# Small filler products in TensorE's gaps in the opening of a kernel of attention, SwiGLU and maxout

## The chip, the cores and the metric

The kernel runs on one core of one Trainium2 chip. The metric is the time of one execution on the device in microseconds (us). PE is TensorE's matmul, PEld its weight load, DVE is VectorE, ACT is ScalarE, POOL is GpSimd, SPq is SyncE's queue, which issues the DMA transfers.

## The reference

Three layers follow one another. The attention has 4 batches of 8 heads with 576 positions of 64 values; half of the heads see the last 32 positions, the other half every 32nd position. Its 2304 rows of 512 values go through a gated layer of width 1536 and then through a layer that takes the largest of three products of width 768.

```python
scores = scale * np.matmul(q, k.transpose(0, 1, 3, 2))
...
attn = np.exp(scores)
attn = attn / (np.sum(attn, axis=-1, keepdims=True) + 1e-09)
return np.matmul(attn, v).astype(np.float32)
...
silu = g * (1.0 / (1.0 + np.exp(-g)))
val = x @ w_val
return (silu * val @ w_out).astype(np.float32)
...
h = np.maximum(np.maximum(x @ w1, x @ w2), x @ w3)
return (h @ w_out).astype(np.float32)
```

All of it is float32. The weights arrive as 64-bit words, and a part of the kernel's work turns each of their tiles into two tiles whose sum it is; each large product is made of three products of such halves.

## The kernel before, in words

The rows are worked on in five chunks of up to 512. While the first chunk's attention is computed, the first layer's weights are still coming in and being converted; this is the opening, and it is written out by hand as a list of steps, `FIRST`. A step is a letter and a number, and each engine runs its own instructions in the order of that list. After the opening a planner orders the instructions.

The steps that matter here are those of the attention blocks. Blocks 0 to 3 belong to the strided heads and blocks 4 to 7 to the local ones. For a block n:

- `l` and `m` load its queries, keys and values; `k0` and `k1` load the constants (identity and masks).
- `Sn` makes the scores on PE: 8 products of 64 rows (line 390).
- `Mn` masks them and takes the row's extreme on DVE (L426), `En` is the exponential on ACT (L434), `Rn` the reciprocal of the sums on DVE (L439, L440), `Nn` the division on POOL (L444).
- `Tn` transposes the result on PE (L456): 2 transposes for a strided block, 4 for a local one. `Vn` copies them out of PSUM, on DVE (L463) or, for blocks 1 and 4, on ACT (L461).
- `Pn` multiplies with the values on PE (L498): 8 products. `Hn` and `Ln` split the outcome into the halves xh and xl (ACT L510 or DVE L512, and DVE L516).

The other letters are the weights' steps: `r` loads a tile, `a`, `q`, `s`, `c`, `t`, `d` convert it on ACT, POOL and DVE (L199 to L228), `h` and `o` split it (ACT L243, DVE L248). `G` and `b` are the gate's first products (L693 to L695 on `ps_g`).

PSUM has eight banks, and each of `Sn`, `Tn` and `Pn` asks for the next one in a rotation (`bank`); it waits until what was in that bank has been read. PE's order in the opening is S0 S1 S2 S3 T0 S4 T1 P0 T2 P1 S5 T3 P2 P3 S6 T4 T5 S7 P5 P4 G0 T6 T7 P6 P7, then S8 and the dense products of the first layer.

Of the kernel before, what the change touches and what calls it, by code (L numbers as in the profile page):

```python
# [7 lines left out]
F32 = mybir.dt.float32  # L8
# [44 lines left out]


FIRST = """
l0 k0 l1 l2 l3 l4 m4 k1 l5 m5 r0 l6 m6 l7 m7 r1 r2 r3 r4 S0 M0 S1 E0 M1 S2 R0 E1 N0 M2 S3 E2 R1 T0 M3 N1 S4 V0
E3 R2 T1 P0 N2 M4 V1 T2 R3 P1 E4 V2 N3 H0 S5 L0 T3 H1 M5 P2 V3 E5 L1 P3 R4 N4 H3 a0 S6 R5 q0 c0 L3 T4 H2 M6 N5
s0 t0 T5 L2 E6 S7 d0 V5 h0 M7 P5 V4 R6 E7 P4 o0 N6 G0 a1 R7 H5 N7 T6 H4 L5 a2 l8 L4 c1 T7 V6 q1 s1 r5 V7 q2 P6
c2 a3 P7 t1 H6 r6 q3 s2 L6 S8 H7 d1 s3 L7 c3 m8 h1 b0 t2 r7 a4 o1 q4 d2 a5 B0 t3 c4 r8 h2 M8 c5 u0 o2 s4 r9 w0
E8 d3 G1 x0 r10 h3 t4 t5 z0 o3 q5 y1 d4 a6 j0 s5 B1 R8 s6 l9 h4 d5 u1 r13 o4 q7 h5 N8 q6 w1 c6 O0 r12 a7 o5 s7  # L60
t6 x1 c7 m9 a8 d6 q8 r11 T8 t7 c8 z1 G2 V8 d7 h6 y3 j1 h7 o6 a9 o7 q9 r14 P8 s8 a10 c9 S9 u2 t8 l10 l11 H8 B2
s9 M9 c10 y4 L8 a11 d8 E9 w2 c11 r15 t10 O1 x2 h8 q11 R9 m10 m11 o8 z2 N9 r17 q10 t9 s11 T9 j2 G3 s10 d9 r16
t11 V9 d10 h9 d11 y7 a12 o9 h10 P9 h11 s12 B3 y6 u3 o10 H9 o11 q12 L9 c12 W10 a13 w3 y9 q13 c13 a14 t12 M10
M11 s13 x3 c14 O2 r21 q14 s14 z3 t13 E10 d12 r18 d13 G4 j3 h12 R10 h13 r19 o12 a15 N10 q15 t14 y10 a16 T10 o13
u4 B4 d14 V10 w4 c15 r20 s15 c16 t15 q16 s16 h14 y12 d15 P10 a17 o14 q17 O3 x4 c17 H10 l12 h15 t16 r23 s17 L10
z4 d16 E11 y13 o15 G5 h16 j4 q18 R11 m12 l13 m13 o16 a18 r24 s18 N11 t17 c18 a19 T11 d17 S12 u5 y15 t18 c19 B5
V11 w5 h17 M12 q19 r22 o17 a20 d18 E12 t19 s20 P11 y16 x5 G6 c20 h18 R12 H11 t20 z5 N12 s19 L11 r26 j5 q20 T12
o18 a21 O4 d20 r25 V12 d19 q21 h20 c21 h19 o20 r27 s21 t21 P12 S13 o19 a22 B6 d21 H12 l14 l15 u6 c22 L12 y19
h21 s22 w6 q22 o21 q23 r28 t22 O5 a24 x6 s23 c24 m14 m15 d22 z6 y18 q24 s24 h22 j6 a23 o22 G7 r29 a25 M13 c23
q25 t24 E13 r31 t23 c25 d24 W14 s25 d23 y21 B7 h24 R13 M14 h23 N13 u7 y22 o23 E14 w7 t25 T13 M15 r32 a26 o24  # L70
O6 V13 R14 s26 x7 q26 c26 r30 a27 N14 z7 t26 q27 d25 P13 r33 a28 j7 G8 h25 d26 H13 o25 s27 L13 c27 y24 h26 c28
t27 a29 T14 o26 q29 r34 B8 d27 V14 s28 u8 s29 c29 w8 y25 t28 h27 q28 t29 o27 a30 O7 r35 x8 s30 q30 d28 z8 y27
c30 h28 j8 a31 o28 q31 G9 d29 q32 y28 s31 c31 t30 h29 t31 E15 d30 O8 d31 u9 o29 h30 R15 h31 o30 a32 N15 y30
a33 w9 B9 s32 q33 o31 a34 c32 y31 q34 c33 s33 t32 T15 a35 x9 c34 G10 V15 t33 s34 z9 d32 q35 j9 h32 d33 s35 P14
P15 o32 u10 B10 t34 h33 w10 c35 H14 H15 d34 L14 L15 h34 o33 O9 o34 y33 x10 t35 z10 d35 y34 j10 h35 G11 o35 y35
O10 u11 w11 B11 x11 z11 j11
"""


# [14 lines left out]
def tile_attention_swiglu_maxout(  # L94
# [13 lines left out]
    nc = tc.nc  # L108
# [6 lines left out]
    def sub(stack, name, bufs, **kw):  # L115
        return stack.enter_context(tc.tile_pool(name=name, bufs=bufs, **kw))
# [9 lines left out]
    const = sub(one, "const", 1)  # L126
# [16 lines left out]
    consts = [cst[:, sum(cols[:i]):sum(cols[:i + 1])] for i in range(len(cols))]  # L143
    minus_half = const.tile([128, 1], F32, name="mh")
    nc.gpsimd.memset(minus_half, -0.5)
    ident, mask, smask = consts[0], consts[2:4], consts[1::3]
    halves = slice(0, sum(cols[:2])), slice(sum(cols[:2]), sum(cols))

# [148 lines left out]
            xt[c] = tuple(x_p.tile([128, NK, N], F32R, name=f"x{p}", tag=f"x{p}{c % 2}") for p in "hl")  # L297
        return xt[c]

    early_banks = [0]  # L300

    def claimed():
        with ExitStack() as tied:
# [5 lines left out]
    class Block:  # L309
# [8 lines left out]
            self.half = [slice(j * D, (j + 1) * D) for j in range(2)]  # L318

        def bank(self):  # L320
            if self.early:
                early_banks[0] += 1
                p, tag = ((acc, "acc"), (gv, "gv"), (acc, "acc"), (att, "att"))[early_banks[0] % 4]
            else:
                p, tag = att, "att"
            return p.tile([128, 512], F32, name="ps_a", tag=tag)
# [202 lines left out]
    def strided_block(srcs, b, g, stacked=False):  # L529

        _, rows, nr = ON_PE[b]
        assert STRIDE % nr == 0

        def dst(src, us):
            su = src.rearrange("p a (r i) -> p a r i", i=rows)
            gs = g[us]
            for c, i0, i1, o in pieces(b * NI, b * NI + rows):
                def part(t):
                    t = t[:, 2:4, :width(c)].rearrange("p a (i r) -> p a r i", r=STRIDE)
                    return t[:, :, gs[0] * nr:(gs[-1] + 1) * nr, i0:i1]  # L540

                xh, xl = x_tile(c)
                yield part(xh), part(xl), su[:, :, :, o:o + i1 - i0]

        at = g[0] // 2 if stacked else g[0]
        return Block(srcs, at, rows * nr, [smask[b]] * len(g), dst, nq=rows * nr, stacked=stacked)

    def pairs(ns):
        ns = list(ns)
        return [ns[i:i + 2] for i in range(0, len(ns), 2)]  # L550
# [89 lines left out]
    def attention_blocks(c):  # L640
        rows = ORDER[ROWS[c]:ROWS[c + 1]]
        blocks = [local_block(g) for g in joined([r // LR for r in rows[::LR]])]
        if c == 1:
            blocks += [strided_block((st1qk, st1v), 1, g) for g in pairs(range(STRIDE // ON_PE[1][2]))]
        return blocks
# [273 lines left out]
    run, h2 = {}, {}  # L919
# [93 lines left out]
    if True:  # L1013
        blocks = [strided_block((st0,), 0, g, True) for g in pairs(range(STRIDE // ON_PE[0][2]))]
        blocks += [local_block(g, (wo_p, wo_p, wo_p, wv_p)[n]) for n, g in enumerate(pairs(range(EARLY)))]
        blocks += attention_blocks(1)

        def evictor(i):
            return nc.vector if i in (0, 2, 3, 5, 6, 7) else nc.scalar

# [2 lines left out]
            "l": lambda i: blocks[i].load_qk(),  # L1023
            "m": lambda i: blocks[i].load_v(),
            "S": lambda i: blocks[i].scores(),
            "W": lambda i: blocks[i].scores_beside(blocks[i + 1]),
            "M": lambda i: blocks[i].least(),
            "E": lambda i: blocks[i].exps(),
            "R": lambda i: blocks[i].inverse(),
            "N": lambda i: blocks[i].normalise(nc.gpsimd if i < 8 else nc.vector),  # L1030
            "T": lambda i: blocks[i].turn(),
            "V": lambda i: blocks[i].evict(evictor(i)),
            "P": lambda i: blocks[i].outputs(),
            "H": lambda i: blocks[i].high(nc.vector if i in (0, 3) else nc.scalar),
# [211 lines left out]
```

## Time and profile before

| | us |
|---|---|
| median of 3 runs | 790.94 |
| lowest and highest | 790.83, 791.69 |
| the profiled execution | 791.56 |
| its span, from the first to the last instruction | 789.5 |
| PE busy in the span | 774.3 |

The profile is that of one execution. Its own time is 0.62 us above the median and 2.06 us above its span. PE busy counts a matmul from its start to its modelled end, so matmuls in a row overlap in it.

### The profile page before, as it was taken

The page shows a single profiled execution, that of the slowest core. Times are in us where ns is not written, and L with a number is a line of the kernel's source. Part 1 is how long each engine was busy: PE and PEld are TensorE (multiplying, and loading weights), DVE is VectorE, ACT ScalarE, POOL GpSimd, SP SyncE. Part 2 cuts the span into 40 slices and gives each one's busy share as a digit, 9 for nine tenths or more (in the row PEclk, how much of TensorE's full clock was granted, in tenths as well). Part 3 has the DMA queues.
Part 4 walks back from the last instruction along what each step waited for, and adds up shares of the span by engine and source line. Part 5 has one row for each costly group of instructions (what it writes and reads, how often), then busy time and mean ns, then how long its engine had stood idle before and what let it go on. Part 6 is the DMA issues. An engine that isn't in the chain of part 4 may idle for free.

```text
span 789.5 us, 13319 instructions
## 1 busy us (share of the span) xinstructions
PE 774.3 (98%) x4642; PEld 711.5 (90%) x4642; DVE 613.1 (78%) x1206; ACT 403.8 (51%) x927; POOL 231.2 (29%) x225
## 2 busy tenths in 40 slices
PE   6999999999999999999999999999999999999998
PEld 4777788888888998988999999999999999999998
DVE  5899998886799999799795778745689377856683
ACT  6899997346474637545342645433245233443331
POOL 2433342022321432324242646521124011321120
PEclk9899999999999999999999999999999999999999
DMA  9989886985846886747788999996775966878722
GB/s 292 328 287 332 300 345 235 360 269 184 276 168 222 302 294 220 250 170 255 253 274 289 302 379 384 345 383 249 274 262 196 423 254 246 286 283 344 271 96 81
DMA packets 75595, 216.26 MB, mean 274 GB/s; under 512 B 8488, under 2 KB 42024, under 8 KB 70920
## 3 DMA queue, kind: packets, MB, share of 16 engines
q1 hardware_dynamic: 75528, 215.41, 76.9%
q8 instruction: 37, 0.61, 0.3%
q14 instruction: 30, 0.25, 0.1%
HBM read 171.34 MB, written 44.04 MB: 273 GB/s over the span
## 4 chain that ended last, share of the span: by engine, by line
PE 79%; DVE 11%; ACT 6%; DMA 2%; issue 2%; SPq 0%; DVEq 0%; ACTq 0%
PE ps_a L850 19%; PE ps_c L850 10%; PE ps_b L850 5%; PE ps_g L693 5%; PE ps_v L693 5%; PE ps_y L694 5%; PE ps_y L693 5%; PE ps_y L695 5%; PE ps_g L695 5%; PE ps_g L694 5%; PE ps_v L695 5%; PE ps_v L694 5%; DVE pr L594 2%; DVE pr L616 2%; DVE stsc L597 1%
## 5 line engine op out<-in xcount | busy, mean ns | idle before, releaser
L729 POOL TENSOR_TENSOR hl<-ht,hh 128x448 fp32r<-128x448 f32 x47 | 61.2, 1303 | 212.4 <-ACT hh L725 195.2
L861 ACT ACTIVATE s<-ps_a 128x384 f32<-128x384 f32 x99 | 48.4, 489 | 134.9 <-PE ps_a L850 134.9
L693 PE MATMUL ps_g<-xh,wh_g 128*128 128x448 f32 (+1 forms) x240 | 91.0, 379 | 2.0 <-ACT ht L712 2.0
L693 PE MATMUL ps_v<-xh,w_v 128*128 128x448 f32 (+1 forms) x240 | 90.6, 377 | 0.4 <-ACT ht L712 0.3
L694 PE MATMUL ps_g<-xl,wh_g 128*128 128x448 f32 (+1 forms) x240 | 90.0, 375 | 0.3 <-DVE xl L516 0.3
L695 PE MATMUL ps_g<-xh,wl_g 128*128 128x448 f32 (+1 forms) x240 | 89.7, 374 | 0.0
L694 PE MATMUL ps_y<-hl,w_o 128*128 128x448 f32 (+1 forms) x240 | 89.6, 373 | 0.0
L695 PE MATMUL ps_y<-hh,w_o 128*128 128x448 f32 (+1 forms) x240 | 89.2, 372 | 0.0
L695 PE MATMUL ps_v<-xh,w_v 128*128 128x448 f32 (+1 forms) x240 | 89.2, 372 | 0.0
L694 PE MATMUL ps_v<-xl,w_v 128*128 128x448 f32 (+1 forms) x240 | 88.8, 370 | 0.0
L693 PE MATMUL ps_y<-hh,w_o 128*128 128x448 f32 (+1 forms) x240 | 83.5, 376 | 0.0
L725 ACT ACTIVATE hh<-ht 128x448 fp32r<-128x448 f32 (+1 forms) x60 | 35.3, 589 | 85.5 <-DVE ht L719 74.9
L800 POOL TENSOR_TENSOR rT<-t,rT 128x384 f32<-128x384 f32 x9 | 12.5, 1392 | 149.3 <-DVE rT L799 149.3
L850 PE MATMUL ps_a<-y0hT,wr 128*128 128x384 f32 x162 | 54.9, 339 | 0.0
L850 PE MATMUL ps_a<-y1hT,wr 128*128 128x384 f32 x162 | 54.5, 337 | 0.0
L693 PEld LDWEIGHTS ps_g<-xh,wh_g 128*128 128x128 f32 x240 | 45.3, 189 | 8.7 <-ACT ht L712 3.1
L693 PEld LDWEIGHTS ps_v<-xh,w_v 128*128 128x128 f32 x240 | 45.1, 188 | 6.4 <-ACT ht L712 0.7
L694 PEld LDWEIGHTS ps_g<-xl,wh_g 128*128 128x128 f32 x240 | 45.4, 189 | 5.3 <-DVE xl L516 0.7
L695 PEld LDWEIGHTS ps_g<-xh,wl_g 128*128 128x128 f32 x240 | 45.4, 189 | 4.9
L693 PEld LDWEIGHTS ps_y<-hh,w_o 128*128 128x128 f32 x240 | 45.1, 188 | 5.2
L892 DVE TENSOR_TENSOR s<-ps_c,s 128x384 f32<-128x384 f32 x36 | 20.0, 556 | 38.2 <-ACT s L861 32.5
L695 PEld LDWEIGHTS ps_v<-xh,w_v 128*128 128x128 f32 x240 | 45.0, 188 | 5.0
(256 smaller groups left out, 2109.3 us busy)
## 6 DMA issues: line engine op xcount, KB each, us to landing
wr<-wsdr SPq DMA_DIRECT2D x36, 1792.0 KB, 8.4
raw<-in_w_dram SPq DMA_DIRECT2D x60, 512.0 KB, 6.7
w_v<-wvdr SPq DMA_DIRECT2D x48, 512.0 KB, 4.6
w_o<-wodr SPq DMA_DIRECT2D x48, 512.0 KB, 4.8
wsdr<-whi SPq DMA_DIRECT2D x36, 256.0 KB, 4.2
wvdr<-w_v SPq DMA_DIRECT2D x12, 512.0 KB, 4.1
wodr<-w_o SPq DMA_DIRECT2D x12, 512.0 KB, 5.8
wsdr<-w SPq DMA_DIRECT2D x24, 256.0 KB, 3.8
```

The lines of the kernel that those rows point to most:

```text
L594: eng.tensor_tensor(pv, self.k[:, 0:i + 1, :], self.q[:, r:r + 1, :].to_broadcast([128, i + 1, D]), ALU.mult)
L597: nc.vector.tensor_reduce(self.sc[:, r, 0:i + 1], pv, AX.X, ALU.add)
L616: eng.tensor_tensor(pv, self.v[:, :, 0:i + 1], self.sc[:, r:r + 1, 0:i + 1].to_broadcast([128, D, i + 1]), ALU.mult)
L693: nc.tensor.matmul(ps, wh, xh, start=first, stop=False)
L694: nc.tensor.matmul(ps, wh, xl, start=False, stop=False)
L695: nc.tensor.matmul(ps, wl, xh, start=False, stop=last)
L725: return nc.scalar.activation(hs[c, f][0], t, AF.Copy).ins
L729: return eng.tensor_tensor(hl, t, f32(hh), ALU.subtract).ins
L800: nc.gpsimd.tensor_tensor(b12, self.raw["B22"], b12, ALU.subtract)
L850: nc.tensor.matmul(ps, w[:, c, a, ks], b, start=first and n == q == 0, stop=last and n == len(wts) - 1 and q == 2, skip_group_check=True,)
L861: nc.scalar.activation(s, ps, AF.Copy)
L892: nc.vector.tensor_tensor(s, ps, s, ALU.add)
```

## The change

A tile of ones, 128 by 128 float32, is set by DVE at the start. A new step `Fn` takes the bank that the next block step would have taken, writes n products of the ones into its first 64 columns, and leaves the bank in a list, from which the next block step takes it and overwrites it. Twelve such steps stand in `FIRST`, with 44 products: 12 before S0, 2 before S1, 1 each before S2, S3 and S4, 6 before P3, 2 before S6, 5 before T4, 6 before T5, 5 before P5, 1 before T7 and 2 before P7. The other steps and their order are the same.

```diff
-l0 k0 l1 l2 l3 l4 m4 k1 l5 m5 r0 l6 m6 l7 m7 r1 r2 r3 r4 S0 M0 S1 E0 M1 S2 R0 E1 N0 M2 S3 E2 R1 T0 M3 N1 S4 V0
-E3 R2 T1 P0 N2 M4 V1 T2 R3 P1 E4 V2 N3 H0 S5 L0 T3 H1 M5 P2 V3 E5 L1 P3 R4 N4 H3 a0 S6 R5 q0 c0 L3 T4 H2 M6 N5
-s0 t0 T5 L2 E6 S7 d0 V5 h0 M7 P5 V4 R6 E7 P4 o0 N6 G0 a1 R7 H5 N7 T6 H4 L5 a2 l8 L4 c1 T7 V6 q1 s1 r5 V7 q2 P6
...
+l0 k0 l1 l2 l3 l4 m4 k1 l5 m5 r0 l6 m6 l7 m7 r1 r2 r3 r4 F12 S0 M0 F2 S1 E0 M1 F1 S2 R0 E1 N0 M2 F1 S3 E2 R1
+T0 M3 N1 F1 S4 V0 E3 R2 T1 P0 N2 M4 V1 T2 R3 P1 E4 V2 N3 H0 S5 L0 T3 H1 M5 P2 V3 E5 L1 F6 P3 R4 N4 H3 a0 F2 S6
+R5 q0 c0 L3 F5 T4 H2 M6 N5 s0 t0 F6 T5 L2 E6 S7 d0 V5 h0 M7 F5 P5 V4 R6 E7 P4 o0 N6 G0 a1 R7 H5 N7 T6 H4 L5 a2
+l8 L4 c1 F1 T7 V6 q1 s1 r5 V7 q2 P6 c2 a3 F2 P7 t1 H6 r6 q3 s2 L6 S8 H7 d1 s3 L7 c3 m8 h1 b0 t2 r7 a4 o1 q4 d2
...
+    ones = const.tile([128, 128], F32, name="ones")
+    nc.vector.memset(ones, 1.0)
...
-    early_banks = [0]
+    early_banks, busy_banks = [0], []
...
         def bank(self):
+            if busy_banks:
+                return busy_banks.pop()
...
+        def keep_busy(n):
+            ps = blocks[0].bank()
+            for _ in range(n):
+                nc.tensor.matmul(ps[:, :64], ones, ones[:, :64], start=True, stop=True)
+            busy_banks.append(ps)
...
+            "F": keep_busy,
```

## Rows read from the trace of the kernel before

**Rows 1.** The page: span, busy us of each engine

```profile
span 789.5 us, 13319 instructions
...
PE 774.3 (98%) x4642; PEld 711.5 (90%) x4642; DVE 613.1 (78%) x1206; ACT 403.8 (51%) x927; POOL 231.2 (29%) x225
```

**Rows 2.** Windows: busy us and instructions by engine, granted clock, DMA share, GB/s

```profile
3.90:9.80 5.90, 4.38 (x64) 3.72 (x64) 2.52 (x28) 4.00 (x23) 0.91 (x2) 1.00 1.03 331
9.80:14.00 4.20, 4.20 (x48) 2.85 (x50) 2.44 (x22) 3.11 (x18) 1.55 (x3) 1.00 1.05 303
...
15.80:20.80 5.00, 2.49 (x43) 1.86 (x42) 4.93 (x28) 4.88 (x20) 2.27 (x3) 1.00 1.02 353
20.90:27.70 6.80, 6.75 (x58) 5.60 (x58) 4.30 (x18) 6.12 (x19) 3.57 (x5) 0.50 1.04 356
...
35.00:54.00 19.00, 19.00 (x112) 15.17 (x110) 18.49 (x40) 18.31 (x45) 6.87 (x9) 1.00 1.02 333
54.00:206.00 152.00, 151.04 (x961) 125.93 (x960) 131.57 (x300) 108.00 (x247) 42.23 (x47) 1.00 0.80 281
```

**Rows 3.** Timeline of PE, opening: start, length (us), instruction, idle before it

```profile
10.44 1.54 PE L390 MATMUL ps_a<-qke 64*64 64x96 f32 x16
11.91 0.69 PE L456 MATMUL ps_a<-cst,raw 128*128 128x128 f32 x2
...
14.19 0.84 PE L390 MATMUL ps_a<-qke 64*64 64x96 f32 x16
...
16.72 0.48 PE L498 MATMUL ps_a<-raw 64*64 64x64 f32 x16 [0.92 <-DVE raw L463]
...
18.59 0.64 PE L456 MATMUL ps_a<-cst,qke 128*96 128x128 f32 x4 [0.63 <-POOL qke L444]
20.20 0.64 PE L456 MATMUL ps_a<-cst,qke 128*96 128x128 f32 x4 [0.97 <-POOL qke L444]
20.77 1.45 PE L390 MATMUL ps_a<-qke 64*64 64x96 f32 x16
22.27 1.98 PE L498 MATMUL ps_a<-qke,ve 96*64 96x64 f32 x32
...
28.69 1.28 PE L498 MATMUL ps_a<-qke,ve 96*64 96x64 f32 x32 [0.34 <-DVE qke L463]
```

**Rows 4.** Chain that ended last, in order of time: start, length, what

```profile
21.63 0.60 DVE qke L463
...
22.27 1.98 PE ps_a L498 x32
...
25.41 0.43 PE ps_g L695
...
55.57 0.23 PE ps_g L694
```

**Rows 5.** Timeline of DVE, opening

```profile
5.07 0.23 DVE L426 CUSTOM_DVE_ANT_0 raw<-ps_a,cst 128x64 f32<-128x64 f32 x1 [5.07 <-PE ps_a L390]
...
13.90 0.42 DVE L463 COPY raw<-ps_a 128x256 f32<-128x256 f32 x1 [0.69 <-PE ps_a L456]
...
23.27 0.66 DVE L248 TENSOR_TENSOR wl_g<-w,wh_g 128x512 fp32r<-128x512 f32 x1
...
27.95 1.28 DVE L463 COPY qke<-ps_a 96x512 f32<-96x512 f32 x2 [2.13 <-PE ps_a L456]
```

**Rows 6.** Timeline of ACT, opening

```profile
12.64 0.38 ACT L461 ACTIVATE raw<-ps_a 128x256 f32<-128x256 f32 x1 [0.99 <-PE ps_a L456]
...
15.54 0.38 ACT L434 ACTIVATE qke<-qke,state 128x96 f32<-128x96 f32 x1 [0.52 <-DVE state L426]
...
29.43 0.39 ACT L510 ACTIVATE xh<-ps_a 128x256 fp32r<-128x256 f32 x1 [1.87 <-PE ps_a L498]
```

**Rows 7.** Timeline of POOL, opening

```profile
0.77 0.16 POOL L588 MEMSET stsc<- 128x72 f32 x1
...
25.00 0.83 POOL L444 TENSOR_TENSOR qke<-qke,state 128x384 f32<-128x384 f32 x1 [0.38 <-DVE state L440]
```

More of the change, by code (lines that the diff above doesn't have):

```diff
@@ L55 @@
 FIRST = """
-l0 k0 l1 l2 l3 l4 m4 k1 l5 m5 r0 l6 m6 l7 m7 r1 r2 r3 r4 S0 M0 S1 E0 M1 S2 R0 E1 N0 M2 S3 E2 R1 T0 M3 N1 S4 V0
-E3 R2 T1 P0 N2 M4 V1 T2 R3 P1 E4 V2 N3 H0 S5 L0 T3 H1 M5 P2 V3 E5 L1 P3 R4 N4 H3 a0 S6 R5 q0 c0 L3 T4 H2 M6 N5
-s0 t0 T5 L2 E6 S7 d0 V5 h0 M7 P5 V4 R6 E7 P4 o0 N6 G0 a1 R7 H5 N7 T6 H4 L5 a2 l8 L4 c1 T7 V6 q1 s1 r5 V7 q2 P6
-c2 a3 P7 t1 H6 r6 q3 s2 L6 S8 H7 d1 s3 L7 c3 m8 h1 b0 t2 r7 a4 o1 q4 d2 a5 B0 t3 c4 r8 h2 M8 c5 u0 o2 s4 r9 w0
-E8 d3 G1 x0 r10 h3 t4 t5 z0 o3 q5 y1 d4 a6 j0 s5 B1 R8 s6 l9 h4 d5 u1 r13 o4 q7 h5 N8 q6 w1 c6 O0 r12 a7 o5 s7
@@ L61 @@
[L61 to L75, printed above, removed]
@@ L76 @@
-O10 u11 w11 B11 x11 z11 j11
+l0 k0 l1 l2 l3 l4 m4 k1 l5 m5 r0 l6 m6 l7 m7 r1 r2 r3 r4 F12 S0 M0 F2 S1 E0 M1 F1 S2 R0 E1 N0 M2 F1 S3 E2 R1
+T0 M3 N1 F1 S4 V0 E3 R2 T1 P0 N2 M4 V1 T2 R3 P1 E4 V2 N3 H0 S5 L0 T3 H1 M5 P2 V3 E5 L1 F6 P3 R4 N4 H3 a0 F2 S6
+R5 q0 c0 L3 F5 T4 H2 M6 N5 s0 t0 F6 T5 L2 E6 S7 d0 V5 h0 M7 F5 P5 V4 R6 E7 P4 o0 N6 G0 a1 R7 H5 N7 T6 H4 L5 a2
+l8 L4 c1 F1 T7 V6 q1 s1 r5 V7 q2 P6 c2 a3 F2 P7 t1 H6 r6 q3 s2 L6 S8 H7 d1 s3 L7 c3 m8 h1 b0 t2 r7 a4 o1 q4 d2
+a5 B0 t3 c4 r8 h2 M8 c5 u0 o2 s4 r9 w0 E8 d3 G1 x0 r10 h3 t4 t5 z0 o3 q5 y1 d4 a6 j0 s5 B1 R8 s6 l9 h4 d5 u1
@@ new lines @@
+r13 o4 q7 h5 N8 q6 w1 c6 O0 r12 a7 o5 s7 t6 x1 c7 m9 a8 d6 q8 r11 T8 t7 c8 z1 G2 V8 d7 h6 y3 j1 h7 o6 a9 o7 q9
+r14 P8 s8 a10 c9 S9 u2 t8 l10 l11 H8 B2 s9 M9 c10 y4 L8 a11 d8 E9 w2 c11 r15 t10 O1 x2 h8 q11 R9 m10 m11 o8 z2
+N9 r17 q10 t9 s11 T9 j2 G3 s10 d9 r16 t11 V9 d10 h9 d11 y7 a12 o9 h10 P9 h11 s12 B3 y6 u3 o10 H9 o11 q12 L9
+c12 W10 a13 w3 y9 q13 c13 a14 t12 M10 M11 s13 x3 c14 O2 r21 q14 s14 z3 t13 E10 d12 r18 d13 G4 j3 h12 R10 h13
+r19 o12 a15 N10 q15 t14 y10 a16 T10 o13 u4 B4 d14 V10 w4 c15 r20 s15 c16 t15 q16 s16 h14 y12 d15 P10 a17 o14
@@ new lines @@
+q17 O3 x4 c17 H10 l12 h15 t16 r23 s17 L10 z4 d16 E11 y13 o15 G5 h16 j4 q18 R11 m12 l13 m13 o16 a18 r24 s18 N11
+t17 c18 a19 T11 d17 S12 u5 y15 t18 c19 B5 V11 w5 h17 M12 q19 r22 o17 a20 d18 E12 t19 s20 P11 y16 x5 G6 c20 h18
+R12 H11 t20 z5 N12 s19 L11 r26 j5 q20 T12 o18 a21 O4 d20 r25 V12 d19 q21 h20 c21 h19 o20 r27 s21 t21 P12 S13
+o19 a22 B6 d21 H12 l14 l15 u6 c22 L12 y19 h21 s22 w6 q22 o21 q23 r28 t22 O5 a24 x6 s23 c24 m14 m15 d22 z6 y18
+q24 s24 h22 j6 a23 o22 G7 r29 a25 M13 c23 q25 t24 E13 r31 t23 c25 d24 W14 s25 d23 y21 B7 h24 R13 M14 h23 N13
@@ new lines @@
+u7 y22 o23 E14 w7 t25 T13 M15 r32 a26 o24 O6 V13 R14 s26 x7 q26 c26 r30 a27 N14 z7 t26 q27 d25 P13 r33 a28 j7
+G8 h25 d26 H13 o25 s27 L13 c27 y24 h26 c28 t27 a29 T14 o26 q29 r34 B8 d27 V14 s28 u8 s29 c29 w8 y25 t28 h27
+q28 t29 o27 a30 O7 r35 x8 s30 q30 d28 z8 y27 c30 h28 j8 a31 o28 q31 G9 d29 q32 y28 s31 c31 t30 h29 t31 E15 d30
+O8 d31 u9 o29 h30 R15 h31 o30 a32 N15 y30 a33 w9 B9 s32 q33 o31 a34 c32 y31 q34 c33 s33 t32 T15 a35 x9 c34 G10
+V15 t33 s34 z9 d32 q35 j9 h32 d33 s35 P14 P15 o32 u10 B10 t34 h33 w10 c35 H14 H15 d34 L14 L15 h34 o33 O9 o34
@@ L77 @@
+y33 x10 t35 z10 d35 y34 j10 h35 G11 o35 y35 O10 u11 w11 B11 x11 z11 j11
 """
```

## The prediction

> **What bounds the kernel now.** I read the page first, then windows over the opening, then the timelines of PE, DVE, ACT and POOL there, and last the chain of waits. PE is busy for 774.3 of 789.5 us [rows 1], so there are 15 us to gain at most, and 3.9 of them pass before the first data land. In the window rows the five engines stand in the order PE, PEld, DVE, ACT, POOL, then comes the granted clock. From 35 us on PE has no gap (19.00 of 19.00 us, then 151.04 of 152) [rows 2]. So whatever reaches PE earlier at about 30 us moves the rest of the kernel forward by as much, as long as DVE and ACT, which are also at 18.5 and 18.3 of 19.0 us there, can come along.
>
> What is not full is the opening, and there the clock matters. From 20.9 to 27.7 us the granted clock is 0.50, the lower of its two levels (1.2 of 2.4 GHz) [rows 2]. Before it fell PE was busy for 2.49 of 5.00 us, with gaps of 0.92, 0.63 and 0.97 us, ended by DVE and POOL [rows 2, 3]. The column shows 1.00 from the start, but the same 16 score records last 1.54 us at 10.44, 0.84 at 14.19 and 1.45 at 20.77 [rows 3]. I take it that PE ran at the lower level from the start too, until shortly before 14.19, and that the column has no record there. Before that rise PE was busy for 4.20 of 4.20 us, and before that for 4.38 of 5.90 [rows 2]. A stretch without gaps came before the rise, one half empty before the fall.
>
> The chain shows that the cold stretch costs something: DVE's copy V5 ends at 22.23, then PE alone is the chain until DVE's next copy at 27.95, which waited 2.13 us for it; ACT's xh at 29.43 waited 1.87 us for PE [rows 4 to 6].
>
> **The change part by part.** *One filler product.* The trace has none. The nearest is P5 with P4: 16 products, also 64 columns wide, in 32 records at the lower level, 1.98 us [rows 3]. A float32 product leaves two records, and two products that use different columns of the array run side by side; so 1.98 is 16 steps of 0.124, and a filler, which has the whole array, takes two steps: 0.25 us at the lower level and half of it, 0.125, at the upper. Lower bound: its two steps overlap like those side by side, 0.12 and 0.06. Upper bound: the two transposes at 11.91, with a full 128 by 128 weight load each, take 0.69 us, 0.35 a record [rows 3]; two records would be 0.69 at the lower level and, halved, 0.35 at the upper. I take 0.25 and 0.125, since the width is the same.
>
> The Trainium skill's page "TensorE: Matmul & The Clock Gate", section "LDWEIGHTS (loading the stationary operand)", says that a load's time is its columns over 1.2 GHz; an estimate from it is 0.107 us for the ones, twice a product, so 0.21 us a filler at the upper level. By that the five before P5 would take 1.07 us and overrun their gap by about 0.5, and the sum below would be 1.9 instead of 2.4. No row here has a load of 128 columns beside a stream of only 64, so neither is shown.
>
> *The ones.* A memset on DVE, which does nothing until 5.07 [rows 5]. The nearest is POOL's memset of 72 columns, 0.16 us [rows 7]; for 128 I take 0.3 us. It is hidden by the wait for the first data, and the ones are ready at about 1.0.
>
> *F12.* 12 x 0.25 = 3.0 us, from 1.0 to 4.0; S0's data are there at 3.90. Cost 0.1 us at S0, and DVE's and ACT's first steps wait for that. Bounds 1.5 us (nothing on the path) and 8.3 us (S0 starts 5.4 us late). *F2, F1, F1, F1* stand in gaps before S1 to S3 that end with transfers, and before S4: 0.5 and 0.25 us, hidden.
>
> *F6 before P3, F2 before S6, F5 before T4, F6 before T5.* At the upper level 0.75, 0.25, 0.63 and 0.75 us in gaps of 0.92, none, 0.63 and 0.97 [rows 3]. They need the bank that the next step needs anyway, so they can start when PE has finished the step ahead. F2 moves S6 by 0.25 us, and with it T4 by as much; its copy V4 is made at 22.2 on ACT, far later. Cost nothing; with these 2.4 us PE would be busy for some 4.8 of the 5.0 us before 20.8 where it was for 2.49.
>
> *F5 before P5.* With the clock up S7 takes 0.88 instead of 1.45 us and ends at 21.65. P5 must wait for V5 until 22.23 [rows 4]. Five fillers take 0.63 of the 0.58 us: cost 0.05.
>
> *The late gain, if the clock stays up.* P5 with P4 takes 1.0 instead of 1.98 us and ends at 23.3. The six gate products step by 0.43 us at the lower level and by 0.23 at the upper [rows 4]; six take 1.4 and end at 24.7, or 24.9, as the third needs the low half of the weights, which DVE has at 23.93 [rows 5]. T6 (0.64 at the upper level, as the same form at 18.59) ends at about 25.5. T7 needs POOL's division, which ends at 25.83 [rows 7]; F1 fits before it. T7 ends at 26.4. DVE copies T6 from 25.8 on, T7 from 26.45 to 27.1, where the two copies ran from 27.95 to 29.23: 2.1 us earlier. P6 runs at 26.5, and F2 before P7 is covered by the second copy. ACT's xh could start at 27.0, but ACT has other work until 27.56, which is 29.43 less its wait of 1.87. So ACT sets the gain: 1.87 us.
>
> *The early gain, if the clock is up by about 10 us.* ACT waits 0.99 us at 12.64 for a transpose and 0.52 at 15.54 for DVE, which in turn waited 0.69 at 13.90 for PE [rows 5, 6]. All of it gone gives 1.5 us more; nothing gone gives 0. PE has long gaps before S1 to S3 that one or two fillers do not close, so the level may well rise only a little before 14; I take 0.6.
>
> *Sum.* -1.87 - 0.6 + 0.05 (F5) + 0.1 (F12), so -2.3 us. Against the profiled execution's 791.56 that is 789.2; that execution is 0.62 above the median, so beside the median the forecast is 788.6.
>
> **The rivals.** A measurement of this kernel can tell about 0.2%, 1.6 us, from no change.
>
> *Held only in part.* The clock falls all the same but later or for less time, or the fillers overrun their gaps because of the weight loads. Some of the 1.87 us is left: a gain of 0.2 to 1.6, about 790.0. For it: with the clock up the same steps take half as long, so new gaps open, and there is no filler before T1, P0, T2, P1, S5, T3 or P2.
>
> *The change doesn't do what it says.* The level is the same in every stretch, the fillers lie in the gaps, or the 2 us are eaten by DVE, ACT or the transfers, whose share is at or above 1.02 until 54 us [rows 2]. Time 790.9. Against it: nothing in the chain from 22 to 30 us is a transfer, and the engines' idle times there end with PE.
>
> *Slower.* The clock falls at 20.9 as before. Then S7 ends at 22.22 with no gap before P5, and the five fillers lie on the chain at the lower level: 5 x 0.25 = 1.25 us; F1 adds 0.25 and F2 up to 0.25 beyond the 0.34 us gap before P6 and P7 [rows 3]. +1.7 us, 792.6. It decides from the point where the level is 0.50 at 22.2. With the upper bound of 0.69 a product it would be +3.5 or more, and F12 would add its 5.4 us at S0: up to 800.
>
> **How the numbers follow.** Forecast (level up through P5 to T7, gain 1.6 to 3.5 us): 0.52, since PE's fill before the fall goes from half to over nine tenths, near that of the stretch that brought the rise. Held in part: 0.22. No effect: 0.14. Slower: 0.12, of which 0.02 within 0.2%. So faster by over 0.2% 0.52; within it 0.22 + 0.14 + 0.02 = 0.38; slower 0.10. The forecast's own range is 787.4 to 789.3. The range reaches to the part-held and the unchanged case, 787.4 to 791.3, and leaves out the slower one and the far end of the early gain.
>
> **What the profile after would show.** Right: a granted clock of 1.00 from 20.9 to 27.7; P5 with P4 in about 1.0 us; gate products 0.23 apart; ACT's wait before xh of L510 at about 27.5 gone; fillers 0.125 us each at the upper level, their last one before P5 ending at about 22.2; PE without gaps from about 29.5. Wrong: a stretch at 0.50 that holds P5; fillers over 0.2 us each at the upper level; S0 later than 4.1; or an opening 2 us shorter and an unchanged end, which would put the loss after 54 us, where the planner, which orders what follows the opening, may have placed instructions otherwise.

## The result and the profile after

The changed kernel takes 795.82 us (median of 5 runs, 795.03 to 797.01) where the kernel before takes 790.94 (5 runs, 790.20 to 792.16): the ratio is 1.0064, its 95% interval 1.0051 to 1.0078. It is slower by about 5 us; 788.6 was forecast. The profiled execution of after took 795.03.

The page after, the lines that answer to [rows 1]:

```profile
span 793.2 us, 13496 instructions
...
PE 784.2 (99%) x4730; PEld 722.4 (91%) x4730; DVE 613.6 (77%) x1207; ACT 404.1 (51%) x927; POOL 232.0 (29%) x225
```

PE is busy for 9.9 us more, and the span is 3.7 us longer. (Before's profiled execution lay 0.6 above its median, after's 0.8 below; that is why the spans differ by less than the medians.)

The windows after, the same stretches as [rows 2]; columns as there:

```profile
3.90:9.80 5.90, 5.90 (x50) 5.43 (x49) 0.84 (x11) 1.44 (x8) 0.00 (x0) 1.00 0.98 312
...
15.80:20.80 5.00, 5.00 (x98) 4.24 (x92) 4.71 (x27) 4.75 (x22) 1.38 (x2) 1.00 1.04 358
20.90:27.70 6.80, 6.80 (x99) 6.31 (x96) 5.46 (x28) 5.33 (x22) 2.23 (x3) 1.00 1.04 355
...
35.00:54.00 19.00, 17.85 (x105) 13.91 (x104) 18.83 (x45) 17.69 (x37) 7.43 (x9) 1.00 0.96 318
```

The granted clock is 1.00 from 20.9 to 27.7 us, where it was 0.50. So the fillers were followed by what they were put in for, and PE has no gap before 27.7 either; that the fillers did it is not shown by this alone. But between 3.90 and 9.80 DVE has done only 0.84 us of work where it had done 2.52: the opening begins late. And from 35 to 54 us PE is now busy for 17.85 of 19.00.

The timeline of PE after (start, length, instruction, idle before it). The line numbers of the block steps are 4 higher than before; L1025 is the filler:

```profile
1.05 5.38 PE L1025 MATMUL ps_a<-ones 128*128 128x64 f32 x24 [1.05 <-DVE ones L147]
6.37 1.12 PE L394 MATMUL ps_a<-raw 64*64 64x64 f32 x16
7.42 1.11 PE L1025 MATMUL ps_a<-ones 128*128 128x64 f32 x4
...
13.78 1.35 PE L394 MATMUL ps_a<-qke 64*64 64x96 f32 x16
15.06 0.44 PE L460 MATMUL ps_a<-cst,raw 128*128 128x128 f32 x2
...
18.05 1.55 PE L1025 MATMUL ps_a<-ones 128*128 128x64 f32 x12
19.53 0.47 PE L502 MATMUL ps_a<-raw 64*64 64x64 f32 x16
19.93 0.66 PE L1025 MATMUL ps_a<-ones 128*128 128x64 f32 x4
...
22.93 1.45 PE L1025 MATMUL ps_a<-ones 128*128 128x64 f32 x12
...
25.55 1.33 PE L1025 MATMUL ps_a<-ones 128*128 128x64 f32 x10
26.81 1.15 PE L502 MATMUL ps_a<-qke,ve 96*64 96x64 f32 x32
...
30.76 0.69 PE L502 MATMUL ps_a<-qke,ve 96*64 96x64 f32 x16 [0.17 <-DVE qke L467]
...
38.95 0.50 PE L697 MATMUL ps_g<-xh,wh_g 128*128 128x512 f32 x1 [1.15 <-DVE ht L756]
```

In the trace of before, S0 and the first product of the second tile of `ps_g`, called the second gate below, stand at:

```profile
3.90 1.12 PE L390 MATMUL ps_a<-raw 64*64 64x64 f32 x16 [3.90 <-DMA raw<-in_st_dram]
...
35.61 0.50 PE L693 MATMUL ps_g<-xh,wh_g 128*128 128x512 f32 x1
```

The twelve fillers before S0 end at 6.4 us, not at 4.0, and S0 starts at 6.37 instead of 3.90. The two before S1 take 1.1 us. S4 is 3.34 us late (13.78 against 10.44), P3 2.81 (19.53 against 16.72), P5 4.54 (26.81 against 22.27). From there the upper level gives back: P6 is 2.07 late (30.76 against 28.69). Then PE waits 1.15 us for DVE at 38.95, a wait that the trace of before does not have; there the same product started at 35.61, so it is 3.34 late. At 85 us the delay is 3.6, and it is 3.6 at 750 us too: the whole loss arises in the opening.

The instructions of DVE, ACT, POOL and SP stand in the same order in both traces, but for the `ones`, and those of PE too but for the fillers. The planner has changed nothing.

### The profile page after: what moved, and what is told of

It reads as the page before. It is cut to its first block, busy times and chain, and to the rows that moved or that the text cites. A ratio compares the mean times of both kernels' runs of the same rounds, so it can differ in the third digit from the quotient of the medians.

```text
span 793.2 us, 13496 instructions
## 1 busy us (share of the span) xinstructions
PE 784.2 (99%) x4730; PEld 722.4 (91%) x4730; DVE 613.6 (77%) x1207; ACT 404.1 (51%) x927; POOL 232.0 (29%) x225
## 4 chain that ended last, share of the span: by engine, by line
PE 79%; DVE 14%; ACT 5%; issue 2%; DMA 0%; DVEq 0%; ACTq 0%
PE ps_a L854 19%; PE ps_c L854 10%; PE ps_b L854 5%; PE ps_v L697 4%; PE ps_y L698 4%; PE ps_y L699 4%; PE ps_y L697 4%; PE ps_g L697 4%; PE ps_v L699 4%; PE ps_v L698 4%; PE ps_g L699 4%; PE ps_g L698 4%; PE ps_a L1025 2%; DVE pr L598 2%; DVE pr L620 2%
## 5 line engine op out<-in xcount | busy, mean ns | idle before, releaser
L697 PEld LDWEIGHTS ps_y<-hh,w_o 128*128 128x128 f32 x240 | 45.1, 188 | 5.2
L699 PEld LDWEIGHTS ps_y<-hh,w_o 128*128 128x128 f32 x240 | 45.1, 188 | 5.0 <-DVE w_o L250 0.3
```

The costliest lines, as they stand in the source:

```text
L697: nc.tensor.matmul(ps, wh, xh, start=first, stop=False)
L699: nc.tensor.matmul(ps, wl, xh, start=False, stop=last)
```

## The experiments

All times below stand beside runs of the kernel before that shared the chip (medians 790.4 to 791.0); ratios are to these, with their 95% intervals. They are not the quotients of the medians and differ from those by up to 0.1%.

### What a filler's time consists of

Two kernels have the change's counts with another shape of filler. In the first the weights are half as wide, in the second the streamed operand is.

```diff
-nc.tensor.matmul(ps[:, :64], ones, ones[:, :64], start=True, stop=True)
+nc.tensor.matmul(ps[:64, :64], ones[:, :64], ones[:, :64], start=True, stop=True)
```

> The changed kernel with fillers that use 64 columns of the ones as weights in place of 128, and so write 64 partitions; counts as in the change. Theory L (the full weight load sets the 0.45 us of a filler at the lower level): a filler takes about 0.25, as wide as the products of P5, F12 ends near 4.0 and S0 is at most 0.2 us late; time about 791. Rival S (the columns that stream through set it): still 0.45, F12 ends at 6.4, time 795.8.

```diff
-nc.tensor.matmul(ps[:, :64], ones, ones[:, :64], start=True, stop=True)
+nc.tensor.matmul(ps[:, :32], ones, ones[:, :32], start=True, stop=True)
```

> The changed kernel with 32 columns of ones streamed in place of 64, with the full weights; counts as in the change. Theory L: a filler still takes 0.4 or more at the lower level, S0 still about 2.2 us late. Rival S: half, 0.22, F12 ends at 3.8 and S0 is not late; time about 790.5.

PE's first rows with weights of 64 columns:

```profile
1.05 2.82 PE L1025 MATMUL ps_a<-ones 128*64 128x64 f32 x24 [1.05 <-DVE ones L147]
4.13 1.12 PE L394 MATMUL ps_a<-raw 64*64 64x64 f32 x16 [0.26 <-DMA raw<-in_st_dram]
```

PE's first rows with 32 streamed columns and full weights:

```profile
1.05 5.33 PE L1025 MATMUL ps_a<-ones 128*128 128x32 f32 x24 [1.05 <-DVE ones L147]
6.31 1.12 PE L394 MATMUL ps_a<-raw 64*64 64x64 f32 x16
```

Half the weights' columns: 2.82 us for the twelve, 0.24 each. Half the streamed columns: 5.33, as with all of them (5.38). The records of the weight loads (PEld) show the same: 24 of them take 2.63 us with 64 columns, 5.20 in the changed kernel. So the load of the 128 columns of weights sets a filler's time here, as theory L said, and the columns that stream do not. (Narrow weights also write half the partitions; that goes with them and is not told apart.) The times follow: 790.90, ratio 0.9993 (0.9975 to 1.0010), and 794.90, ratio 1.0055 (1.0033 to 1.0076). Narrow weights alone take the whole loss away.

### Which fillers cost

Four kernels leave out groups of fillers.

```diff
-... r4 F12 S0 M0 F2 S1 E0 M1 F1 S2 ...
+... r4 S0 M0 F2 S1 E0 M1 F1 S2 ...
```

> Only the twelve fillers before S0 are left out; the other 32 stay. Theory A (the fillers cost twice what the prediction took, and those on the path set the loss; F12 alone makes S0 2.5 us late): S0 starts at 3.9 again, F2 before S1 still takes 1.0 us, and the time falls by 2.0 to 3.0 us against the changed kernel, to about 793.2. Rival B (F12's delay is covered by waits for data, and the fillers from P3 on set the loss): S0 at 3.9, but the time stays within 0.7 us of the changed kernel, about 795.5.

Measured 793.53, ratio 1.0034 (1.0021 to 1.0046): 2.3 us less than the changed kernel, as theory A said. In its profile S0 starts at 4.06, when its data are there.

```diff
-... r4 F12 S0 M0 F2 S1 ... F2 S2 ... F2 P7 ...
+... r4 F12 S0 M0 S1 ... S2 ... P7 ...
```

> Only the twelve fillers before S0 are kept, the other eleven groups left out. Theory A: S0 at 6.4, then S1 to S3 run without waiting for data and win back a part; the lower clock comes back between 20 and 28 us; 1 to 2.5 us slower than before, about 792.5. Rival B: S0 at 6.4, but no later than 0.3 us at the copies of about 14 us; time as before, 790.9.

Measured 790.83, ratio 1.0008 (0.9995 to 1.0021). The time is that of rival B. PE's rows with F12 alone:

```profile
6.36 3.38 PE L393 MATMUL ps_a<-raw 64*64 64x64 f32 x64
10.46 0.44 PE L459 MATMUL ps_a<-cst,raw 128*128 128x128 f32 x2 [0.72 <-POOL raw L447]
```

S0 is 2.46 us late as in the changed kernel, but the 64 score records of S0 to S3 now run in one piece of 3.38 us, since their data have come meanwhile; the first transposes start at 10.46, 0.64 late (9.82 before). The clock helped too: four blocks of scores at the lower level would take 4.2 us, an estimate from steps of 1.05 us between them in the changed kernel, and the transposes at 10.46 take 0.44 as at the upper level. Theory A's lower level between 20 and 28 us did not come back either.

```diff
-... M3 N1 F1 S4 V0 ... F6 P3 ... F2 P7 ...
+... M3 N1 F1 S4 V0 ... P3 ... P7 ...
```

> Only the 17 fillers before P3's are kept: 12 before S0, 2 before S1 and 1 each before S2, S3 and S4. Theory U (F12's delay of 2.5 us can be made good as long as the gaps before S1 to S3 are empty; filled, they carry it on): T0 3 us late, and 1.5 to 2.5 us slower than before, where F12 alone gave 0.6. Rival V (the groups' costs simply add up): 0.6 for F12 and about 1.0 for the four small ones, 1.6 in all, with T0 less than 1.5 us late.

Measured 794.35, ratio 1.0039 (1.0025 to 1.0054). PE's rows with the early fillers alone:

```profile
6.36 1.12 PE L394 MATMUL ps_a<-raw 64*64 64x64 f32 x16
...
13.78 1.55 PE L394 MATMUL ps_a<-qke 64*64 64x96 f32 x16
15.25 0.64 PE L460 MATMUL ps_a<-cst,raw 128*128 128x128 f32 x2
15.82 0.47 PE L502 MATMUL ps_a<-raw 64*64 64x64 f32 x16
```

With 0.7 to 1.1 us of fillers between them S0 to S3 did not catch up: S4 starts at 13.78, 3.34 late, where with F12 alone it starts at 10.83. Up to 0.8 us of that difference, by the estimate above, is the clock, which here was still at the lower level. The mechanism is theory U's, not V's, but the loss (3.1 us by the ratio, 3.8 by the medians) is above what either expected.

```diff
-... r4 F12 S0 M0 F2 S1 ... F1 S4 ... F6 P3 ...
+... r4 S0 M0 S1 ... S4 ... F6 P3 ...
```

> Only the 27 fillers from P3 on are kept. Theory A: at the upper level 0.25 us a filler, so that P5 comes some 1.5 us late; the clock stays up after 20 us and gives back 1.9 or more: within 1 us of before, 790.0 to 791.5. Rival B (these set the loss): 793.5 or more.

Measured 792.21, ratio 1.0020 (1.0005 to 1.0035), between the two expectations. P3, S7, the fillers before P5 and P5 itself in this kernel:

```profile
16.81 0.47 PE L502 MATMUL ps_a<-raw 64*64 64x64 f32 x16
...
22.03 0.88 PE L394 MATMUL ps_a<-qke 64*64 64x96 f32 x16
22.84 1.33 PE L1025 MATMUL ps_a<-ones 128*128 128x64 f32 x10
24.09 1.15 PE L502 MATMUL ps_a<-qke,ve 96*64 96x64 f32 x32
```

The five take 1.33 us and P5 starts at 24.09, 1.8 late, as theory A had it; what theory A got wrong is the gain afterwards. The fillers before S6, T4 and T5 do not fit their gaps either: from P3 to S7 it takes 5.22 us here and 4.05 in the kernel before (16.72 to 20.77). The early group's 0.39% and the late group's 0.20% make 0.59% of the 0.64%: within their intervals the two groups account for the loss.

```diff
-F12 S0  F2 S1  F1 S2  F1 S3  F1 S4  F6 P3  F2 S6  F5 T4  F6 T5  F5 P5  F1 T7  F2 P7
+F6 S0   F1 S1                       F3 P3  F1 S6  F2 T4  F3 T5  F2 P5         F1 P7
```

> About half the counts: 6 before S0, 1 before S1, 3 before P3, 1 before S6, 2 before T4, 3 before T5, 2 before P5, 1 before P7, none at the other four places. Theory A: with 0.45 us at the lower and 0.25 at the upper level F6 ends at about 3.8, so S0 is not late and the rest fits its gaps; if the clock holds, 1.5 to 2 us faster than before, about 789.2; if it falls, as before. Rival C (the clock's 1.9 us is not worth anything later, since DVE or ACT takes it back): 790.9 with the clock up.

Measured 790.38, ratio 0.9991 (0.9978 to 1.0003). PE's rows of it:

```profile
1.05 2.83 PE L1025 MATMUL ps_a<-ones 128*128 128x64 f32 x12 [1.05 <-DVE ones L147]
...
34.13 0.50 PE L697 MATMUL ps_g<-xh,wh_g 128*128 128x512 f32 x1 [1.11 <-DVE ht L756]
```

F6 ends at 3.88, S0 starts at 4.10, and the clock stays up. In this execution the products at 31.56 in the kernel before run 3.03 us earlier. But at 34.13 PE waits 1.11 us for DVE, and after that 1.48 us of the 3.03 are left, against the one execution that had the long stretch at the lower level. The median is not clear of the kernel before. Rival C has the time and a part of the reason.

### Is the lower level part of every execution?

The kernel before, unchanged, was profiled twice more.

> The kernel before, unchanged, profiled once more. Theory A (the cold stretch of 20.9 to 27.7 us belongs to every execution): again 0.50 for some 7 us that hold P5. Rival D (it differs from one execution to the next, and the forecast took one execution for all): the lower level lies elsewhere or is missing, and this execution is then about 1 us shorter than the 791.56 of the first one.

> The kernel before, unchanged, a third look, as the one before. Theory A: 0.50 in a stretch that holds P5. Rival D: the lower level lies elsewhere or is missing.

Windows of the second profile of before (PE, PEld, DVE, ACT, POOL, then the granted clock):

```profile
20.00:23.30 3.30, 3.30 (x45) 2.73 (x45) 2.93 (x15) 2.61 (x11) 0.03 (x1) 0.50 1.04 410
23.40:27.70 4.30, 4.09 (x56) 3.17 (x52) 3.58 (x9) 4.30 (x13) 3.67 (x5) 1.00 1.04 346
```

Windows of its third profile:

```profile
20.00:23.30 3.30, 1.90 (x34) 1.53 (x36) 3.30 (x20) 2.63 (x12) 0.71 (x1) 1.00 1.01 395
23.40:27.70 4.30, 4.02 (x52) 2.96 (x46) 3.43 (x11) 4.30 (x15) 3.21 (x4) 1.00 1.05 318
```

In the second the level is 0.50 until 23.3 us and 1.00 from then on, in the third it does not fall at all. They took 790.85 and 791.42 us, the first one 791.56. So rival D holds in that the forecast took one execution for all; the 1 us that it expected them to be shorter by is 0.7 and 0.1. Yet even the third is not 2 us faster. In it the data for S2 came 1.55 us later than in the first, and there are these rows of PE, P5, P6 and the second gate:

```profile
22.85 1.23 PE L498 MATMUL ps_a<-qke,ve 96*64 96x64 f32 x32 [0.64 <-DVE qke L463]
...
27.03 1.40 PE L498 MATMUL ps_a<-qke,ve 96*64 96x64 f32 x32
...
35.46 0.50 PE L693 MATMUL ps_g<-xh,wh_g 128*128 128x512 f32 x1 [1.13 <-DVE ht L752]
```

The last is the wait for DVE of 1.1 us again, with no filler in the kernel. The second profile has it too:

```profile
34.79 0.50 PE L693 MATMUL ps_g<-xh,wh_g 128*128 128x512 f32 x1 [1.11 <-DVE ht L752]
```

So the first profile, from which the forecast was made, was the odd one: of all profiles of kernels with their clamps, twelve, it alone has no wait here; the other eleven wait 1.10 to 1.16 us. The changed kernel's 38.95 is 4.2 and 3.5 us behind the 34.79 and 35.46 of these two, so its loss is the lateness of its opening and not this wait.

Over all profiles: without fillers from P3 on the level fell around 20 us in two of six; with them in none of eight.

### Where the gain goes

In the kernel with half the counts, DVE's rows before that wait, and POOL's at the same time:

```profile
29.30 1.10 DVE L250 TENSOR_TENSOR w_v<-w,w_v 128x512 fp32r<-128x512 f32 x1
30.32 1.09 DVE L230 CUSTOM_DVE_ANT_0 w<-w,q 128x1024 uint16<-128x1024 uint16 x1
31.34 0.83 DVE L224 TENSOR_SCALAR w<-w 128x512 int32<-128x512 int32 x1
```

```profile
28.73 3.15 POOL L218 TENSOR_SCALAR w<-w 128x512 f32<-128x512 f32 x3
```

Those on POOL are clamps, which limit weights to their range. The three come one right after another, and DVE's three operations beside them take 1.10, 1.09 and 0.83 us. In the first profile of before:

```profile
32.03 0.68 DVE L248 TENSOR_TENSOR w_v<-w,w_v 128x512 fp32r<-128x512 f32 x1
...
33.23 0.41 DVE L222 TENSOR_SCALAR w<-w 128x512 int32<-128x512 int32 x1
```

```profile
32.55 1.58 POOL L216 TENSOR_SCALAR w<-w 128x512 f32<-128x512 f32 x1 [2.85 <-ACT w L199]
```

The same three take 0.68, 0.68 and 0.41 there; a clamp of POOL fell among them only at 32.55, and it was the one that was stretched, to 1.58 us, where a clamp alone takes 0.61 (at 25.92). The Trainium skill's page "SBUF — State Buffer", section "SBUF: two separate sides", says that the two engines share a pair of ports, which the operation that starts first holds for its whole length while the other is blocked; on DVE's side that holds for operations in a two-port mode, or with two inputs from SBUF against an operation of POOL that reads SBUF. The rows agree in that one engine's operation is stretched while the other's runs, on either side; that a lock does it no run here shows. The changed kernel's DVE shows the same:

```profile
34.35 0.84 DVE L250 TENSOR_TENSOR w_v<-w,w_v 128x512 fp32r<-128x512 f32 x1 [0.18 <-ACT w_v L245]
35.11 1.09 DVE L230 CUSTOM_DVE_ANT_0 w<-w,q 128x1024 uint16<-128x1024 uint16 x1
36.13 0.86 DVE L224 TENSOR_SCALAR w<-w 128x512 int32<-128x512 int32 x1
```

The next kernel is that with half the counts, without these three clamps (those weights are not limited to their range).

```diff
-... c3 ... c4 ... c5 ...
+... ... ...
```

> The kernel with half the counts, and three of POOL's clamps left out (weights 3, 4 and 5; those weights are not limited to their range). Theory P (what the opening wins by 28 us is given back because POOL's clamps then run beside DVE's conversions and stretch three of them by 0.4 us each): the three DVE operations at 29 to 32 us take 0.68, 0.68 and 0.42 us, the second gate's products start 1 to 1.3 us earlier than in the kernel with half the counts, and the time falls by about 1 us to 789.4. Rival Q (PE's wait before the second gate comes from DVE's amount of work, not from POOL): that start moves by under 0.4 us, time as with half the counts, 790.4.

DVE's and PE's rows of it:

```profile
31.03 0.69 DVE L250 TENSOR_TENSOR w_v<-w,w_v 128x512 fp32r<-128x512 f32 x1
...
32.23 0.42 DVE L224 TENSOR_SCALAR w<-w 128x512 int32<-128x512 int32 x1
```

```profile
34.62 0.50 PE L697 MATMUL ps_g<-xh,wh_g 128*128 128x512 f32 x1 [0.17 <-DVE ht L756]
```

The three take 0.69, 0.69 and 0.42, PE's wait shrinks from 1.11 to 0.17, and the time is 788.96, ratio 0.9974 (0.9962 to 0.9986). The start itself was not earlier in this execution (34.62 against 34.13), though theory P had expected 1 to 1.3 us. The opening ran later: S2 began 0.36 us behind that of the kernel with half the counts (8.15 against 7.79), and the scores at 15.00 still took 1.02 us where those at 13.43 there took 0.86, so that P3 was 1.72 behind. What moved is the wait and, over all executions, the time; there theory P stands.

To see what the fillers add to that, the kernel before was run without the clamps, and with no filler.

> The kernel before, without any filler, with the same three clamps of POOL left out (weights 3, 4 and 5 are not limited to their range). Theory P2 (the fillers at half the counts are worth nothing, and the gain of 0.26% beside the kernel before is that of the clamps alone): faster than before by 0.15 to 0.35%, about 789.2. Rival F (the fillers keep the clock up, and only then does the room that the clamps leave pay): within 0.1% of before, 790.5.

Measured 788.48, ratio 0.9969 (0.9957 to 0.9981). Its wait of PE:

```profile
33.39 0.50 PE L693 MATMUL ps_g<-xh,wh_g 128*128 128x512 f32 x1 [0.19 <-DVE ht L752]
```

The gain is that of the clamps, as theory P2 said; with fillers it is not larger. This is the fastest kernel of the study, but it leaves a part of the computation out. A kernel that keeps the clamps and runs them at another time was not tried.

The last one has narrow fillers in the late gaps alone, 14 of them (4 before P3, 3 before T4, 4 before T5, 3 before P5; the count of 20 in the expectation is a slip). Each took 0.17 to 0.19 us at the upper level (0.68 for four, 0.56 for three) and not the 0.07 of the expectation.

> Only 20 fillers, before P3, T4, T5 and P5 (4, 3, 4, 3 times three quarters, all with 64 columns of weights), none before 14 us. Theory L (a filler of this width takes 0.07 us at the upper level, all of them lie in gaps): P5 not later than in the kernel before, no lower level after the rise, and up to 1 us faster than before. Rival D (in most executions of the kernel before the lower level is short or missing, so there is little to win): same as before within 0.7 us.

Measured 790.78, ratio 0.9997 (0.9986 to 1.0008), as rival D said. In its profile the clock stays up once it has risen, and the opening is 3.0 us shorter at 33.49 us of the kernel before's first profile, of which 1.2 are lost at this row:

```profile
33.84 0.50 PE L697 MATMUL ps_g<-xh,wh_g 128*128 128x512 f32 x1 [1.11 <-DVE ht L756]
```

So fillers that cost nothing are worth nothing that can be measured here.

## Why the prediction was wrong

*The step that failed most* is the first of "The change part by part": one filler at 0.25 and 0.125 us, "since the width is the same". It is 0.45 at the lower level (5.38 us for 12) and 0.24 to 0.27 at the upper (1.45 for 6, 1.33 for 5). The width that counts is the weights': P5's products load 64 columns, the fillers 128, and with 64 a filler takes 0.24 at the lower level, close to the 0.25 taken. What was measured lies about halfway between the value taken and the upper bound from transposes with the full load. The Trainium skill's page "TensorE: Matmul & The Clock Gate", section "LDWEIGHTS (loading the stationary operand)", which the prediction weighed, says that the columns of the weights set a load's time, and the runs agree. The estimate from it, 0.107 us a load, is near the 0.12 to 0.13 a record measured at the upper level; at the lower level a record takes 0.22.

*F12* was to cost 0.1 us. S0 became 2.47 us late. The rival "Slower" had this as an upper bound, 5.4 us, and the forecast left it out. *F2, F1, F1, F1* were to be hidden: behind a late S0 they took away the gaps in which the scores could have caught up.

*F6, F2, F5 and F6* from P3 to T5 were to cost nothing. They take 1.55, 0.66, 1.33 and 1.45 us where the gaps were 0.92, none, 0.63 and 0.97; with the late fillers alone those from S6 to T5 cost 1.2 us (5.22 against 4.05 from P3 to S7). *F5 before P5* was to cost 0.05 us. It took 1.33, and P5 was 4.54 late in all. A loss of this size was foreseen only with the clock at its lower level. The prediction's estimate of 0.21 us a filler gave an overrun of 0.5 us here, but the forecast did not take it; its "1.9 instead of 2.4" should start from 2.3, the prediction's own sum.

*The late gain* was 1.87 us by ACT and 2.1 by PE and DVE. From P5 to P6 the changed kernel won back 2.47. Against the first profile that step was right; but in the third profile of before, where the level does not fall, P5 to P6 takes 4.18 us without fillers and 3.95 in the changed kernel, so against such an execution there is hardly anything to gain. A part of it went again at the second gate. The prediction held it good "as long as DVE and ACT" can come along, and did not price that DVE's conversions then run beside POOL's clamps, which stretches three of them by 0.2 to 0.4 us each and makes the wait at the second gate.

*The clock*: 1.00 from 20.9 to 27.7 us, as forecast. But the lower level is no fixed cost of the kernel before: one further execution had half of it, one none. *The early gain* did not come: in the changed kernel the fillers did not bring the rise forward. The changed kernel's scores still ran at the lower level at 13.78, though PE had been without a gap from 1.05 us on; with the early fillers alone the rise lay between 15.25 and 15.82, in the kernel before shortly before 14.19, with F12 alone before 10.46. With half the counts it lay between 10.74 and 12.01, and with the same early fillers but without the clamps between 15.00 and 15.95, so one profile does not tell what a set of fillers does to it. What sets the moment of the rise stays open. So does whether the late fillers hold the level: none of eight fell, but four of the six without them did not either.

## What to carry to other kernels

The price of a small product is to be taken from rows with the same width of weights, not with the same width of output: a filler should load few columns. Filler work ahead of data that are about to land should end before them, and fillers behind it also take the slack in which a late start is made good. And a cold stretch seen in one profile is worth a look at further executions, and at what the next engine does when PE gets through earlier, before it is removed.

## What the runs showed of the hardware

A record of a small float32 product (a weight load and its matmul; two for each product) with 128 columns of weights took 0.22 us at the lower clock level (24 in 5.38 us) and 0.12 to 0.13 at the upper (12 in 1.45, 10 in 1.33), whether 64 or 32 columns were streamed; with 64 columns of weights it took 0.12 at the lower level (24 in 2.82). DVE operations of 0.68 us took 1.09 and 1.10 beside POOL's clamps, and a clamp of 0.61 us took up to 1.58 beside DVE's. PE was busy without a gap from 1.05 to 13.78 us and was still at the lower level (16 score records in 1.35 us, 0.86 at the upper).
